# Layer B's values by way of DRAM: one write per block, then one read per quarter of the features and group of partitions, with a new written order

## The chip, the cores and the metric

The kernel runs on one core of one Trainium2 chip. The metric is the device time of one launch in microseconds (us). A core has five instruction queues that run side by side and wait for each other by semaphores: TensorE (PE, with its weight loads PEld), VectorE (DVE), ScalarE (ACT), GpSimd (POOL) and SyncE (SP), which here issues nearly all transfers. Matrix products land in PSUM, of which there are eight banks; everything else works in SBUF, a memory of 128 partitions. DRAM is reached only by transfers.

## The reference

Four layers run in turn, A, B, A, B, each as `x = x + layer(layernorm(x))`, on 2048 positions of width 512 (32 heads of 16 features), all in bf16. Layer A is a linear attention with a softmax feature map. Layer B is a dilated local attention, and the change touches only it:

```python
W, dil = 8, 2
idx = pos[:, None] - (jnp.arange(W) * dil)[None, :]      # positions s, s-2, ..., s-14
logits = jnp.einsum("bhsd,bhswd->bhsw", q, kg) * scale   # kg, vg: k and v gathered at idx
attn = _softmax(jnp.where(mask, logits, -1e9), axis=-1)
o = jnp.einsum("bhsw,bhswd->bhsd", attn, vg)
return o.reshape(B, S, D) @ wo
```

So each position looks at eight positions, two apart, of its own past, in each head.

## The kernel before

The 2048 positions are cut into four blocks of 512. A stage is named by layer pair and block: `b1_01` is the projection of layer B, first pair, block 1. Every stage adds steps to short queues, one for each stage and engine, and a long string `_ORDER` names, in base 36, which queue gives its next step. It was found by a search outside the kernel and fixes the order of every instruction on every engine. `_CHOICE` holds one digit for each step that may run on either of two engines (for most, evictions from PSUM above all, 1 is VectorE and 0 is ScalarE), and `_SLOTS` names the buffer that each tile takes. Nothing is decided when the kernel runs: each engine works through its own list and waits where an operand or a buffer is not there yet.

Seven of the eight blocks of layer B are worked out elementwise (the eighth, block 3 of the second pair, uses TensorE in another way, by `s_e1` to `s_e4`). For one of the seven:

- `s_b1` projects: `mm` (L951) makes Q, K and V in PSUM with its 16 features cut into four quarters of four (partition = 4 times the head + the quarter, and the four features of a quarter side by side in it), and `ev` (L203 on VectorE, L205 on ScalarE) copies them to SBUF. V and K carry 16 columns of the block ahead of it (the halo; POOL copies it, L977 to L993).
- `s_b2` makes the weights: `prod` (L1043) multiplies Q by eight shifted windows of K on VectorE, `lgt` (L1050) sums over features on TensorE, `ex`, `den`, `rd` and `pt` (L1057 to L1078) make the softmax, giving PT, whose partitions are four groups of 32 heads; group g stands for the window offsets g and g + 4.
- `s_b3` applies them: `pav` (L1105) multiplies PT by Vg on VectorE, one instruction for each quarter q of the features, `mo` (L1114) sums over window offsets on TensorE, `ev` copies the sum to oT. `s_out` (L543 to L567) multiplies by the output weights, adds x, and stores or normalizes for the next layer.

Vg is V laid out anew: for quarter q and group g, the 32 partitions 32g to 32g + 31 hold that quarter of the 32 heads, shifted by 2g columns. The step `vrep(q)` (L1012) of the SP queue makes it by four transfers for the four groups, in the order 0, 2, 1, 3, each of 32 rows of 2104 elements, out of every fourth partition of V in SBUF into 32 adjoining partitions of Vg in SBUF. That is 16 transfers to a block and 112 in all. Two quarters share one of the eight large buffers ("big"), which `prod`, `pav` and layer A's tiles use as well. A step `vwr` that writes V to DRAM and a branch of `vrep` that reads it from there in one transfer for all four groups are in the code, but its option, `v_dram`, is empty, so neither runs.

The same SP queue issues, in the written order, the loads, the transposes of the normalized x (`tr`, L473, tile xnT), the round trip of layer A's scales through DRAM (L848 and L855, tile Prho), the block diagonal and DRAM traffic of the eighth block (L1226, L1232 to L1243), and the stores of the output (L567).

Of the kernel before, what the change touches and what calls it, by code (L numbers as in the profile page):

```python
# [19 lines left out]
H = 32  # L20
# [3 lines left out]
NB = 4  # L24
# [5 lines left out]
KVW = 16 + TB  # L30
VGW = 3 * KVW + TB + 8
# [31 lines left out]
4 z 1s s z i 3 1t 1u 21 z z 10 3 1t i7 1v 22 22 21 1 24 24 2p z 0 t u 13 11 15 1t 1t t 16 1w 1t 1y 12 12 12 12  # L63
1x x 1t 5 v w w 25 y 14 2f 2f 18 18 18 18 1z 2g 2c 17 6 19 18 1c 1d 39 2d 1b 1a 2d 22 22 1f 1f g 21 22 22 3a 3a
2c 2c 1f 2d 20 21 1f 22 2c 7 7 20 20 22 26 29 1g 1f 1k 39 3a 2d 2d 2d 2d 1i h 3b 2f 24 2i 1h 1e 29 1j 1l 2q 2h
27 2d 2n 3c 2o 2o 29 29 2a 39 2k 2k 3a 2k 2k 2n 2n 2n 2q 2o 2o 2r 3a 3a 2q 2q 2o 2o 2o 29 2y 2y 2l 2s 2k 2o 2z
2z 2z 2z 31 31 36 3c 33 24 36 36 28 36 2y 2y 2v 2v 2z 2v 37 36 2z 2z 2z 2f 2j 2u 2v 2b 2w 2b 2b 2b 2m 36 2m 36
2m 36 36 2m 39 3a 3b 3b 31 2v 2t 3a 31 32 4e 37 3c 34 35 39 3a 2x 2x 3c 2x 30 2x 38 38 36 38 38 3i 3c 3b 3c 3c
3c 7 3d 3e 3e 3j 3k 3k 3b 3k 3c 3l 5h 3m 3n 3m 3d 3e 3d 3l 5i 3o 3m 3e 3e 3l 3p 3m 3q 3r 3m 3m 5j 3d 3v 5i 3e 3e
3s 3e 20 20 20 20 3t 3m 5h 3u 5n 3m 3m 5m 3d 3e 7c 5h 5q 5o 5p 5r 5k 5i 3f 3g 3g 7 3f 3g 3g 5l 3m 5i 5i 7d 3w 3x  # L70
5i 5i 3z 5i 5i 3f 3f 7e 5i 5s 3g 3y 3g 40 41 7d 5w 42 7f 41 41 7f 41 5t 7f 3g 5v 3g 5u 5x 44 43 45 bd 43 43 46
43 47 5y 3f 43 47 48 90 5x 5x 4b e 49 4c 60 61 41 41 4a 41 41 3g 5x 5z 5z 4d 4g 4g 4h 5z 62 5z 4l 4l 4l 91 92 7d
7d 7g 63 4i 5z 91 4f 4n 4q 4q 4m 4q 63 66 67 64 65 7j 7i 7h 4l 7k 4r 93 4g 4g 4j 4w 4w 7l 7l 4o 4w 7o 68 4k 4q
4u 93 93 4t 4s 4f 7l 7p 7m 7n 4p 4v 7n 7l 7q 6p 6k 6k 4v 6k 7n 7n 91 91 6f 6g 7r 6n 6m 6k 6a 6a 4w 94 6l 7n 69
7r 7u 6o 7v 96 7t 97 4x 95 7s 7w 98 4x 4x 4x 6f 6c 6h 4y 4y 6a 6d 6b 6r 6r 99 6f 6i 6r 99 3h 99 99 9d 9e 3h 6f
6j 6a 6e 9a 9b 9c 9b 6r 9b 9b 83 7y 7y 84 9f 9b 8d 7z 6s 6s 6s 9f 9h 6s 6t 6t 88 89 9i 7y 6s 6t 4w 4x 83 83 6q
6q 7y 6q 85 88 4y 88 8b 83 9g 87 86 81 b2 9j 9k 88 8c 9m 9n 8f 9w 9x 82 9w 9w a1 6r 9z 69 6u 9w 80 6u 6v 8a 6u
6v 6x 6v 4w 6w 6q 6u 6v 6y 9m 4v 4z 4z 6z 4v 70 71 4z 4z 70 70 9y 72 7x 73 72 74 70 75 72 72 76 9o 9r 9r 50 51
8f 50 50 72 52 76 78 8e 8e 50 53 77 54 9r 9u 79 7a 9m 9p 7b 8f 9s 9t 55 8e 56 57 8f 55 58 55 55 59 8g 8g 8g 8e
a0 8g 57 57 a3 9r 5a 57 9v 9m 9q 5b a3 57 5b 8h 8h 5c b3 5e 5d 5f 5g 7x 9l a2 b0 b0 a3 b1 b1 b1 8g 8h b1 b3 b3  # L80
b6 b3 b7 bz c0 c0 a4 a4 a4 a3 a4 a5 a5 bz c0 c0 bz d3 b4 bz c0 c0 c0 c0 8f 8i b0 b1 a4 8i 8i 8i a5 as at b0 b1
b1 bx ap a2 b5 b1 ap 8j 8k 8j 8j 8l 8m 8j bx 8n 8o a3 a6 a2 a6 8p 8o 8o 8o bx aq aq aq aq by by by 8q 8t 8r 8s
as 8q a2 as as bx a6 a7 8q 8q a7 by 8u bz 8q a6 8u 8w 8y by by aw av 8v a7 8x a8 a7 aa ap ap a9 ab ac b8 b8 au
ac i7 ac ac by by bx b8 b8 ad aq aq af aq aq ag b9 bo c0 8z ah b8 bb bb ae ae ae ae ai be ax ae ai aj an c1 be
bc bb bc bc ak ax bc bb bc bc bc bc ac ac am ax ac ax ay al ac bg be bm bm ao bm bm bj bn bn bn bn bn bn ar ax
az az az bu bu bu bu az bn bn c2 bv bj bj by bu bj bu ba ba ba ba bp bh bp bp c1 bq bk bs br be c1 c1 bu bu bu
# [12 lines left out]
ih ic dz ic dw ii ii fi ij gr gr gt ij ik ij ij fj fj ik il ga gu il in gs fl ii ij ij gv ii fj fj im ij ij ik
il ik fn fo gr gr il gw gx iq io iq iq gv gw gv gw gv gv ip iq iv dx dx fk fm fm gy gz h2 is gw gw ir it h2 iw  # L100
iu h0 it ix iw h3 h3 h4 h5 h6 h2 h1 h3 h7 h2 h5 h3 h8 h5 h5
"""


_CHOICE = (
    "0010110111100111111111000000100000100110011100000111011110010100000101010000100000000000111101011100"
    "1010010100001100100000000000000011111110000100001010100000000000000000010111001000001101000000000000"
    "1010000011111100000000000100010110011011010100101111000000001001000000010110010001000100011100100000"
    "00000000011111010000011100000000000000000000000001000011001000000000000000001100"
)  # L110


_SLOTS = {
    "med": (
        "0123456789abcdef346aff72ffc3105f92b4de6a7fd92b317ef99962c0517dbf2e3abf6925cd13e273a31dad901d74235cdb"
        "f72a94d35c017b9264acf31d08"
    ),
    "ps": (
        "0123124350123021456715604156734153267234701623047237452365001230210345672135304675261473045672350146"
        "1401230453013042567103651251741023452036714302310345031240230435406703203501467012012457245201240310"  # L120
        "3245602750235102563740130473024567142362047540123640760437034563745101021345067241301456701236204531"
        "7024560124567326452016435735601247351204561203460750264012312301203405367136731421432102324567467556"
        "47554701213740542010"
    ),
    "big": (
        "012345670123456012345617234561720351724361720436170425361725362503421034210354276"
    ),
    "t2": (
        "0123455500111123334555555555555555000002123402222222221314504555545555444455223000000145523333333333"
        "333333301045234102"  # L130
    ),
    "pp": (
        "640620202020"
    ),
}

# [1 line left out]
class _Fast:  # L138
# [804 lines left out]
    def s_b1(self, L, b):  # L943
        nc, add = self.nc, self.step
        st = "b1_%d%d" % (L, b)
        T = {}
# [52 lines left out]
        def vrep(dl):  # L999
            if dl == 0:  # L1000
                self.Vg[L, b] = {}
            if dl % 2 == 0:
                self.Vg[L, b][dl // 2] = self.big([2, NB * KVW], "Vg")
            if (L, b) in _OPT["v_dram"]:
                a = self.VD[L, b][dl:dl + 1, 2:3]
                src = bass.AP(a.tensor, a.offset, [[2, 4], [4 * NB * KVW, H], [1, VGW]])
                nc.sync.dma_start(out=self.Vg[L, b][dl // 2][:, dl % 2, 0:VGW], in_=src)
                return
            for g in (0, 2, 1, 3):
                a = T["V"][dl:dl + 1, 0:1, 2 + 2 * g:3 + 2 * g]  # L1010
                src = bass.AP(a.tensor, a.offset, [[4 * a.ap[0][0], H], [1, VGW]])
                nc.sync.dma_start(out=self.Vg[L, b][dl // 2][32 * g:32 * g + 32, dl % 2, 0:VGW], in_=src)  # L1012

        if b:
# [507 lines left out]
class _Layout:  # L1522
# [578 lines left out]
```

## Time and profile before

| | |
|---|---|
| median of 3 runs | 328.9 us (328.38 to 330.63) |
| profiled execution | 329.39 us, of which the span of the profile is 327.7 us |
| mean granted TensorE clock | 0.994 |
| transfers of V to Vg | 112 of 131.5 KB, median 4.8 us from issue to landing |

The page of the profile covers one execution. Its first part gives the busy time of each engine, its second the span in 40 equal slices (8.2 us each): one digit for each engine and slice, the busy share in tenths; below them the clock that TensorE was granted, the busy share of the 16 transfer engines, and what they moved. A view by windows gives the same for any stretch. A busy TensorE is not TensorE at its peak, since its products are pipelined.

### The profile page before, as it was taken

Reading aid. Unit: us, or ns where it says so; the run is one execution under the profiler, and the core shown is the slowest. Engines: PE = TensorE matmul, PEld = TensorE weight load, DVE = VectorE, ACT = ScalarE, POOL = GpSimd, SP = SyncE. Lnnn points to the kernel's source line nnn. Section 1 sums busy time; section 2 is a strip of 40 time slices with the busy share of each in tenths; the row PEclk is TensorE's granted clock in tenths of the full one; section 3 lists DMA queues with packets and bytes.
Section 4 is the critical chain, followed back from the end, with each engine's and each line's share of the span. In section 5 each row is a group of like instructions: output and inputs, shape, how many; then the busy total and the mean of one; then the engine's idle time right before and its main releaser. Section 6 shows DMA issues by size and latency. Waiting matters only on the chain.

```text
span 327.7 us, 8877 instructions
## 1 busy us (share of the span) xinstructions
PE 308.8 (94%) x3542; PEld 153.5 (47%) x3574; DVE 296.3 (90%) x456; ACT 278.1 (85%) x640; POOL 39.1 (12%) x64
## 2 busy tenths in 40 slices
PE   7999999899999999999999999789999999986993
PEld 3644456444444454444444455543545444443441
DVE  6899995989999999999999999599898999999493
ACT  4999989999789977999999999799898866987360
POOL 6000000000020006000000000000040395210000
PEclk9999999999999999999999999999999999999799
DMA  7964300023677979679991200050588997549814
GB/s 203 341 162 90 108 2 4 2 68 81 144 172 140 132 149 158 108 131 131 145 121 28 40 0 4 4 141 9 145 147 121 192 136 131 135 83 176 158 67 137
DMA packets 45793, 36.41 MB, mean 111 GB/s; under 512 B 30832, under 2 KB 41136, under 8 KB 45744
## 3 DMA queue, kind: packets, MB, share of 16 engines
q1 hardware_dynamic: 45216, 35.75, 56.2%
q8 instruction: 30, 0.49, 0.7%
q14 instruction: 19, 0.16, 0.2%
q10 hardware_dynamic: 528, 0.02, 0.1%
HBM read 11.13 MB, written 3.25 MB: 44 GB/s over the span
## 4 chain that ended last, share of the span: by engine, by line
DVE 31%; ACT 31%; PE 18%; issue 12%; DMA 3%; SPq 2%; DVEq 0%; ACTq 0%
DVE prod L1043 6%; ACT Eq L729 5%; DVE pav L1105 5%; PE PS L543 5%; ACT sqd L563 5%; ACT Ek L622 4%; DVE x L556 4%; DVE Ek L674 3%; PE PS L951 3%; DVE xn L466 3%; ACT oT L205 2%; PE PS L1050 2%; DVE s L649 2%; ACT xn L468 2%; DMA wraw<-in_A_wqkv_dram 1%
## 5 line engine op out<-in xcount | busy, mean ns | idle before, releaser
L951 PE MATMUL PS<-xnT,WB 128*128 128x512 bf16 x336 | 76.7, 380 | 0.3 <-ACT K L205 0.2
L1105 DVE TENSOR_TENSOR pav<-PT,Vg 128x4096 bf16<-128x4096 bf16 (+1 forms) x29 | 63.3, 2219 | 0.6
L1043 DVE TENSOR_TENSOR prod<-QT,K 128x4096 bf16<-128x4096 bf16 x28 | 62.9, 2285 | 0.4 <-ACT QT L205 0.3
L951 PEld LDWEIGHTS <-WB 128*128 128x128 bf16 x336 | 37.3, 114 | 37.1 <-issue 4.2
L543 PEld LDWEIGHTS <-oT 128*128 128x128 bf16 x240 | 22.5, 98 | 31.3 <-issue 5.6
L729 ACT ACTIVATE Eq<-PS 128x512 bf16<-128x512 f32 x64 | 34.7, 624 | 0.0
L622 ACT ACTIVATE Ek<-PS 128x512 bf16<-128x512 f32 x64 | 33.9, 627 | 0.0
L563 ACT ACTIVATE sqd<-x 128x512 bf16<-128x512 bf16 x48 | 30.4, 633 | 2.1 <-DVE x L556 1.2
L721 PE MATMUL PS<-xnT,WA 128*128 128x512 bf16 x128 | 31.1, 380 | 0.2 <-ACT bs L870 0.2
L543 PE MATMUL PS<-WoB,oT 128*128 128x512 bf16 x105 | 27.7, 393 | 3.1 <-issue 2.9
L616 PE MATMUL PS<-WA,xnT 128*128 128x512 bf16 x124 | 29.9, 379 | 0.5 <-DVE x L556 0.2
L628 PE MATMUL PS<-WA,xnT 128*128 128x512 bf16 x122 | 29.9, 379 | 0.3
L543 PE MATMUL PS<-WoA,oT 128*128 128x512 bf16 x119 | 29.3, 380 | 0.8 <-DVE x L556 0.2
L556 DVE SCALAR_TENSOR_TENSOR x<-PS,x 128x512 bf16<-128x512 f32 x45 | 28.9, 684 | 0.3 <-PE PS L543 0.2
L205 ACT CAST oT<-PS 128x512 bf16<-128x512 f32 (+1 forms) x47 | 24.8, 595 | 3.8 <-PE PS L1114 3.5
L616 PEld LDWEIGHTS <-xnT 128*128 128x128 bf16 x128 | 12.3, 98 | 15.0 <-issue 0.6
L628 PEld LDWEIGHTS <-xnT 128*128 128x128 bf16 x128 | 12.3, 98 | 14.4
L205 ACT CAST V<-PS 128x512 bf16<-128x512 f32 x27 | 15.4, 591 | 4.1 <-PE PS L951 4.1
L674 DVE TENSOR_TENSOR Ek<-Ek,rk 128x4096 bf16<-128x4096 bf16 (+1 forms) x10 | 18.6, 1860 | 0.3 <-ACT rk L669 0.3
L721 PEld LDWEIGHTS <-WA 128*128 128x128 bf16 x128 | 11.7, 97 | 15.2 <-issue 2.0
L205 ACT CAST K<-PS 128x512 bf16<-128x512 f32 x30 | 17.4, 591 | 0.3 <-PE PS L951 0.3
L466 DVE TENSOR_SCALAR xn<-x,rstd,nmr 128x512 bf16<-128x512 bf16 x46 | 16.8, 408 | 0.6
(164 smaller groups left out, 496.9 us busy)
## 6 DMA issues: line engine op xcount, KB each, us to landing
Vg<-V SPq DMA_DIRECT2D x112, 131.5 KB, 4.8
Prho<-rd SPq DMA_DIRECT2D x8, 512.0 KB, 5.4
x<-in_A_x_dram SPq DMA_DIRECT2D x3, 512.0 KB, 5.8
WB<-in_B_wqkv_dram SPq DMA_DIRECT2D x3, 512.0 KB, 8.6
out_dram<-x SPq DMA_DIRECT2D x6, 256.0 KB, 2.3
wraw<-in_A_wqkv_dram SPq DMA_DIRECT2D x4, 256.0 KB, 5.4
vd<-Vs SPq DMA_DIRECT2D x2, 272.0 KB, 3.3
x<-in_A_x_dram SPq DMA_DIRECT2D x4, 128.0 KB, 3.9
```

What stands on the lines that cost most here:

```text
L205: self.nc.scalar.copy(out=out, in_=in_)
L543: nc.tensor.matmul(y[:], lhsT=lh(t, c), rhs=Wo()[:, c, :], start=(c == 0), stop=(c == NB - 1 and not onpe))
L556: nc.vector.scalar_tensor_tensor(out=xb[:, t, :], in0=T[t][:], scalar=1.0, in1=xb[:, t, :], op0=ALU.mult, op1=ALU.add, **kw)
L563: nc.scalar.activation(out=sqd[:], in_=xb[:, t, :], func=ACT.Square, accum_out=T["ss"][:, t:t + 1])
L616: nc.tensor.matmul(pk[:], lhsT=xnT[:, t, k, :], rhs=self.WA[:, k, D:2 * D], start=(k == 0), stop=(k == NB - 1))
L622: nc.scalar.activation(out=T["E"][:, t, s, :], in_=T["k", t][:], func=ACT.Exp, scale=1.0 - 2.0 * s)
L628: nc.tensor.matmul(pv[:], lhsT=xnT[:, t, k, :], rhs=self.WA[:, k, 2 * D:3 * D], start=(k == 0), stop=(k == NB - 1))
L721: nc.tensor.matmul(pq[:], lhsT=self.WA[:, k, hb * P:(hb + 1) * P], rhs=xnT[:, :, k, :], start=(k == 0), stop=(k == NB - 1))
L729: nc.scalar.activation(out=self.Eq[L, b][s][:, :, hb, :], in_=T[hb][:].rearrange("p (t i) -> p t i", t=4), func=ACT.Exp, scale=1.0 - 2.0 * s)
L951: nc.tensor.matmul(pp[:], lhsT=self.WB[:, k, i * D + c:(i + 1) * D:NB], rhs=xnT[:, :, k, :], start=(k == 0), stop=(k == NB - 1))
L1043: nc.vector.tensor_tensor(out=pr[:], in0=QT[:, c:c + 1, :].to_broadcast([P, NW, TB]), in1=win, op=ALU.mult)
L1105: nc.vector.tensor_tensor(out=pv, in0=PT[:, :, lo:lo + n].unsqueeze(1).to_broadcast([P, NB, 2, n]), in1=vw, op=ALU.mult)
```

## The change

The option and the branch go. For all seven blocks `vwr` now writes V with its halo to DRAM in one transfer (128 partitions of 2112 elements, 540 KB), and `vrep(q)` makes the same four transfers of 32 rows for groups 0, 2, 1, 3, with the DRAM copy as their source. A read has to wait until the write has landed. Tile and instruction shapes on the computing engines stay as they are. `_ORDER`, `_CHOICE` and `_SLOTS` are replaced by ones searched for this form, so that nearly every instruction stands at another place of its queue, and some evictions, normalizations and residuals change their engine.

```diff
     "split": ((1, 2), (1, 3)),
-    "v_dram": (),
     "half_mo": (),
...
 _ORDER = """
-8 2e a d c 23 i i i 0 j 9 k j l i 2 i i i i 0 b o p i f 2 0 1m 1m 1o m n i i i i 1n 1m 1m 1p 1q 1m 1r o q r 1m t
...
+8 i i i i i i i i i i i 0 a e 9 j 2 0 b k j o p 23 0 t i i l 1m 2 1m o q i r m 0 t 1n u 1o 3 1t s 1u t 1m x 1m
...
@@ -1001,14 +1000,9 @@
                 self.Vg[L, b] = {}
             if dl % 2 == 0:
                 self.Vg[L, b][dl // 2] = self.big([2, NB * KVW], "Vg")
-            if (L, b) in _OPT["v_dram"]:
-                a = self.VD[L, b][dl:dl + 1, 2:3]
-                src = bass.AP(a.tensor, a.offset, [[2, 4], [4 * NB * KVW, H], [1, VGW]])
-                nc.sync.dma_start(out=self.Vg[L, b][dl // 2][:, dl % 2, 0:VGW], in_=src)
-                return
             for g in (0, 2, 1, 3):
-                a = T["V"][dl:dl + 1, 0:1, 2 + 2 * g:3 + 2 * g]
-                src = bass.AP(a.tensor, a.offset, [[4 * a.ap[0][0], H], [1, VGW]])
+                a = self.VD[L, b][dl:dl + 1, 2 + 2 * g:3 + 2 * g]
+                src = bass.AP(a.tensor, a.offset, [[4 * NB * KVW, H], [1, VGW]])
                 nc.sync.dma_start(out=self.Vg[L, b][dl // 2][32 * g:32 * g + 32, dl % 2, 0:VGW], in_=src)
 
         if b:
@@ -1024,8 +1018,7 @@
             add(st + "kh", "POOL", halo)
         if b < 3:
             add(st + "v", "POOL", vhalo_out)
-        if (L, b) in _OPT["v_dram"]:
-            add(st + "v", "SP", vwr)
+        add(st + "v", "SP", vwr)
         for dl in range(4):
             add(st + "v", "SP", vrep, dl)
```

More of the change, by code (lines that the diff above doesn't have):

```diff
@@ new lines @@
+7d 4g 4g 63 5z 4i 4l 4n 63 67 65 66 64 93 4q 4q 93 93 4j 4w 4w 4t 7g 4g 68 7i 4l 4q 4f 4s 4l 7h 91 91 4k 7k 7j
+4p 4u 7l 7l 7o 7m 4o 6p 7l 7p 7l 7q 3h 94 98 96 97 6a 95 6a 6a 6b 99 99 4w 7n 7n 7n 7n 6c 6f 6f 4w 6g 7r 7n 7r
+7t 7v 7s 9c 6a 7u 9a 9b 9b 99 bo 9d 4v 4v 4v 4v 4v 7w 6h 99 9e 6r 9b 9b 9f 9b 6f 6i 6f 4x 4x 6d 6j 8d 4f 4x 4x
+6k 6l 6e 6k 6m 4y 6r 4y 6k 6k 6o 6n 69 6q 69 9f 9h 9j 9g 6r 4w 9i 9k i7 83 7y 7y 80 4x 6r 6s 6s 6s 7z 4y 6s 6t
+6t 7y 81 7y 6s 6t 3h 88 89 88 83 8a 7x 9w 9x 82 9m 9m 9o 4w 9m 9n 84 8f 83 86 85 88 88 8c 83 87 9p 6q 6q 8b 6r
@@ L110 @@
+    "0001000011111100000000000010010110110011010101010011100000010000000000000110010001000000010101000100"
+    "00000000011111001000011111000000000000000000000000000011000000000000000000000100"
 )
 _SLOTS = {
-    "med": (
[L115 to L123, printed above, removed]
+    "ps": (
+        "0120341250674523106435123467304716230176423072140127143517201341230456724013567142034562317056472310"
+        "2314052316370132012456734025013467501234504623465712032145123143567102403450210210210452102415213421"
+        "0231405605231026542165215236213567156042071402607160170170261206415012012345647012350467151623017245"
+        "3401260123456074367012306273451207345234514230231231230201204250143153605612701405467137245401501454"
+        "23670163701241542301"
+    ),
@@ L124 @@
+    "med": (
+        "0123456789abcdef0043332369a01b3578cdef4293c5deaa0f3c9d214b66af50ed2c659beda10ff2fcbbbed5f78b023ca1b6"
+        "970ed3ca675fbe129ad3c06754"
     ),
     "big": (
[L126 removed]
+        "012345670123456723457230451723046172041573214573214506321406325061325631205310574"
     ),
     "t2": (
[L129 removed]
@@ L130 @@
-        "333333301045234102"
+        "0123455550000011113244444444444444444450513241111111110304521555545551541455533300221145530000000000"
+        "000000021425345014"
     ),
     "pp": (
-        "640620202020"
+        "062626262604"
     ),
```

79 lines of the change are left out of this document (36 added, 43 removed).

## The prediction

> **What bounds the kernel now.** I read the page first: its busy times and its slices.
>
> ```profile
> span 327.7 us, 8877 instructions
> ...
> PE 308.8 (94%) x3542; PEld 153.5 (47%) x3574; DVE 296.3 (90%) x456; ACT 278.1 (85%) x640; POOL 39.1 (12%) x64
> ...
> DVE  6899995989999999999999999599898999999493
> ...
> PEclk9999999999999999999999999999999999999799
> DMA  7964300023677979679991200050588997549814
> ```
>
> Three engines are nearly full, and no transfer queue can be the bound alone, with DMA at 0 in seven slices. DVE's digits are 9 from slice 7 on with few breaks: 5 at slices 6 and 25 (layer A's exponentials, ACT's work), 4 at slice 37, the tail. The view by windows says how full the elementwise part of the first layer B is:
>
> ```profile
> 100.00:120.00 20.00, 19.71 (x122) 9.55 (x113) 18.98 (x24) 18.62 (x41) 0.55 (x2) 1.00 0.90 137
> 120.00:140.00 20.00, 19.86 (x136) 9.15 (x137) 19.79 (x16) 17.36 (x41) 5.88 (x5) 1.00 0.75 133
> 140.00:160.00 20.00, 19.81 (x136) 8.86 (x137) 19.47 (x15) 19.84 (x52) 0.15 (x1) 1.00 0.95 141
> 160.00:180.00 20.00, 19.77 (x165) 8.69 (x166) 19.64 (x23) 19.87 (x47) 1.19 (x3) 1.00 0.64 84
> 200.00:210.00 10.00, 9.17 (x252) 5.72 (x251) 7.16 (x13) 7.61 (x18) 0.00 (x0) 1.00 0.01 3
> 300.00:310.00 10.00, 7.33 (x175) 3.90 (x176) 5.21 (x6) 4.07 (x13) 0.00 (x0) 0.83 0.97 180
> ```
>
> The columns after the length are PE, PEld, DVE, ACT and POOL busy, the granted clock, the DMA share and GB/s. From 100 to 180 us DVE idles 2.1 of 80 us: here time is DVE's work plus what DVE waits. From 300 to 310 us nothing is full but DMA. So the change can act in three ways: less or more work in DVE's queue, a DVE wait for Vg, and the tail.
>
> **The work that moves between engines.** Counting both written orders, instruction by instruction, DVE loses four copies of oT, two of vaug and half a one of kvT, and gains one each of K and xnT, two normalizations xn, one residual x, and one product Eq from PSUM in place of one from SBUF. ACT takes the mirror image.
>
> ```profile
> L203 DVE CAST oT<-PS 128x512 bf16<-128x512 f32 x14 | 9.4, 682 | 0.0
> L466 DVE TENSOR_SCALAR xn<-x,rstd,nmr 128x512 bf16<-128x512 bf16 x46 | 16.8, 408 | 0.6
> L556 DVE SCALAR_TENSOR_TENSOR x<-PS,x 128x512 bf16<-128x512 f32 x45 | 28.9, 684 | 0.3 <-PE PS L543 0.2
> L839 DVE TENSOR_TENSOR Eq<-PS,Eq 128x512 bf16<-128x512 f32 x18 | 11.7, 681 | 0.0
> L839 DVE TENSOR_TENSOR Eq<-bs,Eq 128x512 bf16<-128x512 bf16 x14 | 5.7, 416 | 0.1
> L205 ACT CAST oT<-PS 128x512 bf16<-128x512 f32 (+1 forms) x47 | 24.8, 595 | 3.8 <-PE PS L1114 3.5
> L468 ACT ACTIVATE xn<-x,nmr,rstd 128x512 bf16<-128x512 bf16 x18 | 14.3, 814 | 1.7 <-DVE nmr L457 1.7
> ```
>
> DVE: 4.5 copies fewer, net of the two gained and taking all at oT's 0.682, is -3.1; xn +0.8; x +0.7; Eq +0.3. Sum **-1.3 us**. ACT: four copies more by 0.595, +2.4; two xn fewer, -1.6; a net residual fewer at about a copy's 0.6; sum +0.2, nothing. PE loses one product. So the new order's gain in work is small, and only in DVE's queue.
>
> **The transfers.** The old ones and their nearest relatives, in the page's part on DMA issues and the view of the tile Vg:
>
> ```profile
> Vg<-V SPq DMA_DIRECT2D x112, 131.5 KB, 4.8
> Prho<-rd SPq DMA_DIRECT2D x8, 512.0 KB, 5.4
> out_dram<-x SPq DMA_DIRECT2D x6, 256.0 KB, 2.3
> vd<-Vs SPq DMA_DIRECT2D x2, 272.0 KB, 3.3
> xnT<-xn SPq DMA_TRANSPOSE x11, 4.6
> ```
> ```profile
> L1012 SPq DMA_DIRECT2D Vg<-V x112: 467/592/1782, 91.9 to 304.1; - x112
> ...
> DMA to landing us min/median/max: 2.8/4.8/8.2
> ```
>
> The last number of an issue row is the median from issue to landing; the tile view gives ns that SP takes to issue one (least, median, most). The number of these transfers stays 112; what is added is seven writes of 540 KB, and in front of each block's 16 reads a wait for the write. No row shows such a write. Below stands out_dram's 2.3 us; above, Vs's 3.3 us plus the other 268 KB at the slow rate of the next fence, 135 GB/s, 2.0 us: 5.3. I take 4.4, Vs's 3.3 plus 268 KB at the 247 GB/s at which Prho's rows, as long as these, move there. The rate of the copies themselves:
>
> ```profile
> 106.00:108.00 2.00, 2.00 (x11) 1.03 (x10) 2.00 (x4) 1.97 (x3) 0.00 (x0) 1.00 1.11 135
> 88.00:90.00 2.00, 2.00 (x11) 1.00 (x10) 2.00 (x2) 0.42 (x1) 0.00 (x0) 1.00 0.91 247
> ```
> ```profile
> 118.59 15.74 SPq L1012 DMA_DIRECT2D Vg<-V  x20
> 142.48 5.31 SPq L1012 DMA_DIRECT2D Vg<-V  x8
> ```
>
> SBUF to SBUF, with the engines' share at 1, they move 135 GB/s, while Prho out of DRAM moves 247 (into 128 partitions, not 32). SP's own rows give one copy in 0.66 us (5.31 / 8) to 0.79 us (15.74 / 20), against 0.59 to issue one. A read from DRAM is thus between 0.59 and 0.97 us apart (131.5 KB / 135 GB/s); I take 0.59, because its source is Prho's. [...]
>
> So from V's last eviction to a landed Vg: write 4.4; the first quarter's four reads, last issued 3 x 0.59 later and landed after 2.8 to 4.8: **9.0 to 11.0 us**. The sixteenth: 4.4 + 15 x 0.59 + 2.8 to 4.8 = **16.1 to 18.1**. [...]
>
> **Where that is late.** What covers it is the work standing in DVE's queue between V's eviction and `pav`. For blocks 01 and 11 the new order leaves 5 to 8 us less of it than the old one, two or three large products, although there is now a write to wait for.
>
> ```profile
> L1105 DVE TENSOR_TENSOR pav<-PT,Vg 128x4096 bf16<-128x4096 bf16 (+1 forms) x29 | 63.3, 2219 | 0.6
> L1043 DVE TENSOR_TENSOR prod<-QT,K 128x4096 bf16<-128x4096 bf16 x28 | 62.9, 2285 | 0.4 <-ACT QT L205 0.3
> L1078 DVE TENSOR_TENSOR PT<-E,rden 128x1024 bf16<-128x1024 bf16 x7 | 4.8, 691 | 0.6 <-ACT rden L1073 0.4
> ```
>
> The new order: block 01 has three `prod`, two `pt`, a copy of K and three xn: 3 x 2.29 + 2 x 0.69 + 0.68 + 3 x 0.41 = 10.1 us. First quarter needed at 10.1 (landed at 9.0 to 11.0), the fourth three `pav` later, at 16.8 (16.1 to 18.1): a wait of 0 to 1.3, take **0.6**. Block 11 has block 10's four `pav` and one `pt`, 4 x 2.22 + 0.69 = 9.6; fourth at 16.2: 0 to 1.9, take **0.9**. Blocks 00, 02, 03 and 10 have from 15 to 36 us of such work ahead of the first quarter, and 22 or more ahead of the fourth: hidden under `prod` and other blocks' `pav`, until that cover shrinks by some 4 us. What is behind the wait: SP holds the transpose of block 02's xn behind block 00's sixteen reads, where the old order let it in after eight copies. 4.4 + 16 x 0.59 + 4.6 (xnT's landing) = 18.4 us after V, while the first K product of block 02 stands 18 us of DVE work later: 0 to 1, take **0.3**, since PE has block 01's V there. Behind block 11's reads stand nine of the 16 Qbd transfers for the eighth block; its products come after block 11's `pav` begins, with block 12's projections ahead of them, so nothing, at most the 4.4 us of the write where PE has no other work left.
>
> **The tail.** Rows of the timeline of ACT, PEld and DVE, of the chain of waits, two windows of 1 us, and the transfers from 299.5 to 303 us:
>
> ```profile
> 292.86 0.59 ACT L205 CAST V<-PS 128x512 bf16<-128x512 f32 x1
> 302.62 0.53 PEld L543 LDWEIGHTS <-oT 128*128 128x128 bf16 x3 [2.61 <-issue]
> 302.75 2.29 DVE L1105 TENSOR_TENSOR pav<-PT,Vg 128x4096 bf16<-128x4096 bf16 x1
> ```
> ```profile
> 298.51 1.24 PE PS L1322 x126
> ```
> ```profile
> 303.00:304.00 1.00, 1.00 (x4) 0.39 (x3) 1.00 (x1) 0.00 (x0) 0.00 (x0) 0.55 1.06 160
> 305.00:306.00 1.00, 1.00 (x4) 0.29 (x2) 0.04 (x1) 0.00 (x0) 0.00 (x0) 0.50 1.05 168
> ```
> ```profile
> q8 instruction: 1, 0.02, 2.6%
> ```
>
> Block 12's V is out at 293.45 and its first `pav` starts at 302.75, 9.3 us later, on PT, not Vg. The new order has about the same work of PE there; against 9.0 to 11.0 the wait is 0 to 1.7, take **0.9**. In those 9 us lies a gap of 2.61 us of PE with no releaser, behind 126 short products in 1.24 us, while a 0.02 MB piece of instructions is under way with DMA at a share of 1; then the clock is near 0.50 for 3 us, another 1.5 lost. I read it as PE out of instructions. The new order has three groups of 64 such products in a row where the old had two, with Vg in flight too, so I keep the gap: no term.
>
> **Sum.** -1.3 (DVE) + 0.6 + 0.9 + 0.3 + 0.9 = +1.4 on the profiled execution's 329.39 us: 330.8. That execution lies 0.5 above the median of its runs (328.9), so **330.3 us**, in practice no change. With every read at its lower and upper landing the waits are 0 to 5.9, hence 327.6 to 333.5.
>
> **Rivals**, each counted from 328.9.
> 1. *Slow reads, slower than before.* If 32 partitions of a destination, and not an SBUF source, set the 135 GB/s, the reads stay 0.79 apart as in the 20 of the timeline. Fourth quarter: 4.4 + 15 x 0.79 + 4.8 = 21.1 us; late by 4.3 at block 01 and 4.9 at 11, and the first quarter by 2.3 at the tail: 11.5 - 1.3, about **339**. It decides from a pitch of about 0.67 (with a landing of 3.8, the waits then come to 4.6 us, one per cent above the work saved). For it: the 20 copies ran slower than that. Against: Prho's 247.
> 2. *Reads that free the queue.* At 247 GB/s the 16 reads are done in 8.5 us, the DMA share at the dense products falls, and the gap of 2.6 and the slow clock's 1.5 go with it: -1.3 - 4.1, **323.5**. For it: the gap stands only where DMA is full; against: the new order puts more short products in a row.
> 3. *All hidden* (the change does not reach what ends last). DVE had 0.6 us of idle before all `pav`; if ACT delivers V earlier than its place suggests, only -1.3 is left: **327.6**.
> 4. *The new order loses elsewhere.* Every buffer and nearly every place changed; one more gap as at 200 to 210 us, where DVE idles 2.8 of 10, on top of my +1.4 gives 333; two give 336. I take **334**.
>
> **How the numbers follow.** Forecast 0.38, slow reads 0.21, free queue 0.17, hidden 0.13, lost elsewhere 0.11. The range has to take in most of the free queue and of the slow reads, so 323.5 to 338.0. One per cent is 3.3 us, about what a measurement can tell from no change. Faster by more (under 325.6): nearly all of rival 2, a part of 3, 0.22. Slower by more (over 332.2): rivals 1 and 4, and some of the forecast, 0.35. Between: 0.43.
>
> **What would show it.** Vg<-vd's landing and SP's pitch over 16 reads: 0.59 to 0.66 for me, 0.79 for rival 1. DVE's wait for Vg before L1105 (new line 1098): 2 to 3 us in all, at blocks 01, 11 and 12. vd<-V: 4.4 us. PE's gap without releaser past 290 us: kept, or gone with a clock of 1.00 (rival 2). DVE's busy time: 295.0. I am wrong in kind if DVE waits elsewhere, or if a transpose of xn ends a wait of PE by more than 1 us.

## The result and the profile after

The changed kernel takes 332.2 us in the median of 19 executions, the kernel before 328.6 in the same series. Two of the 19 were disturbed (335.3 and 337.3 us); without them the median is 331.9 us (329.7 to 334.2), and all that follows is compared in this way. The ratio is **1.0098, 95% interval 1.0073 to 1.0123**. The forecast was 330.3, no change; the result is slower by one per cent, at the edge of that. The profiled execution took 333.58 us. Its page, the parts that answer those shown of before:

```profile
span 331.8 us, 8908 instructions
...
PE 313.1 (94%) x3573; PEld 152.9 (46%) x3573; DVE 295.2 (89%) x453; ACT 278.7 (84%) x642; POOL 42.3 (13%) x64
...
PEclk9999999999999999999999999999999999979799
...
q1 hardware_dynamic: 46224, 39.53, 45.1%
...
L1098 DVE TENSOR_TENSOR pav<-PT,Vg 128x4096 bf16<-128x4096 bf16 (+1 forms) x29 | 63.3, 2217 | 3.9 <-DMA Vg<-vd 3.6
...
Vg<-vd SPq DMA_DIRECT2D x112, 131.5 KB, 3.2
...
vd<-V SPq DMA_DIRECT2D x7, 528.0 KB, 3.0
```

DVE's work fell by 1.1 us, the span grew by 4.1. DVE now waits for Vg, 3.6 us in three places. But each transfer became faster: a copy lands in 3.2 us where it took 4.8. The row q1 gives packets, MB and share of the 16 engines' time; the kernel before has

```profile
q1 hardware_dynamic: 45216, 35.75, 56.2%
```

so 3.8 MB more were moved in 11 points less of the engines' time. The clock has two dips to 7 in the last eight slices, where it had one. Where they are, in windows of 2 us (PE, PEld, DVE, ACT, POOL, clock, DMA share, GB/s), with TensorE's two longest waits ahead of them:

```profile
PE PS L1315 <- issue: 2.2, 1, 2.2
PE PS L1271 <- DMA Qbd<-Qs: 2.1, 1, 2.1
```
```profile
294.00:296.00 2.00, 2.00 (x50) 0.91 (x31) 2.00 (x2) 1.86 (x5) 0.00 (x0) 0.62 0.68 110
296.00:298.00 2.00, 2.00 (x6) 0.76 (x5) 2.00 (x2) 0.89 (x3) 1.05 (x1) 0.53 0.21 61
...
308.00:310.00 2.00, 2.00 (x67) 1.20 (x68) 1.81 (x3) 0.61 (x3) 0.00 (x0) 0.53 0.87 283
310.00:312.00 2.00, 2.00 (x7) 0.78 (x6) 2.00 (x2) 0.60 (x1) 0.00 (x0) 0.61 0.51 176
```

Each wait is followed by about 4 us in which TensorE has some 0.57 of its clock: 1.7 us lost each time, beside the wait itself. This execution has both, and its mean clock is 0.990; the mean clocks say that others have less of it. Of after's executions, those with a mean clock of 0.996 or more took 329.7 to 331.1 us, those from 0.992 to 0.995 took 330.7 to 332.6, those with 0.991 or less 332.3 to 334.2.

### The profile page after: what moved, and what is told of

Its sections match the earlier page's. It is cut to its first block, busy times and chain, and to the rows that moved or that the text cites. A ratio compares the mean times of both kernels' runs of the same rounds, so it can differ in the third digit from the quotient of the medians.

```text
span 331.8 us, 8908 instructions
## 1 busy us (share of the span) xinstructions
PE 313.1 (94%) x3573; PEld 152.9 (46%) x3573; DVE 295.2 (89%) x453; ACT 278.7 (84%) x642; POOL 42.3 (13%) x64
## 3 DMA queue, kind: packets, MB, share of 16 engines
q1 hardware_dynamic: 46224, 39.53, 45.1%
## 4 chain that ended last, share of the span: by engine, by line
PE 54%; ACT 16%; DVE 14%; DMA 6%; SPq 4%; issue 4%; DVEq 0%; ACTq 0%
PE PS L950 13%; PE PS L542 9%; PE PS L627 6%; PE PS L720 6%; DVE pav L1098 5%; PE PS L615 5%; DMA Vg<-vd 4%; ACT Eq L728 3%; PE PS L1043 3%; ACT sqd L562 3%; SPq L1006 2%; DVE x L555 2%; ACT Ek L621 2%; ACT oT L204 2%; DMA wraw<-in_A_wqkv_dram 2%
## 5 line engine op out<-in xcount | busy, mean ns | idle before, releaser
L950 PE MATMUL PS<-xnT,WB 128*128 128x512 bf16 x336 | 78.1, 383 | 0.3
L542 PEld LDWEIGHTS <-oT 128*128 128x128 bf16 x240 | 23.2, 100 | 31.5 <-issue 4.7
L728 ACT ACTIVATE Eq<-PS 128x512 bf16<-128x512 f32 x64 | 33.9, 615 | 0.0
L542 PE MATMUL PS<-WoA,oT 128*128 128x512 bf16 x128 | 30.0, 379 | 1.6 <-DVE oT L202 1.5
L204 ACT CAST oT<-PS 128x512 bf16<-128x512 f32 (+1 forms) x51 | 27.5, 596 | 4.6 <-PE PS L1107 3.9
L555 DVE SCALAR_TENSOR_TENSOR x<-PS,x 128x512 bf16<-128x512 f32 x46 | 29.7, 683 | 1.5 <-PE PS L542 1.4
L615 PE MATMUL PS<-WA,xnT 128*128 128x512 bf16 x128 | 30.4, 379 | 0.0
L627 PE MATMUL PS<-WA,xnT 128*128 128x512 bf16 x128 | 30.4, 379 | 0.0
L542 PE MATMUL PS<-WoB,oT 128*128 128x512 bf16 x112 | 29.6, 401 | 0.1
L465 DVE TENSOR_SCALAR xn<-x,rstd,nmr 128x512 bf16<-128x512 bf16 x48 | 17.6, 415 | 0.6
L1107 PE MATMUL PS<-pav,indAV 128*32 128x512 bf16 (+1 forms) x232 | 15.1, 374 | 2.2 <-DVE pav L1098 2.1
```

What stands on the lines that cost most here:

```text
L204: self.nc.scalar.copy(out=out, in_=in_)
L542: nc.tensor.matmul(y[:], lhsT=lh(t, c), rhs=Wo()[:, c, :], start=(c == 0), stop=(c == NB - 1 and not onpe))
L555: nc.vector.scalar_tensor_tensor(out=xb[:, t, :], in0=T[t][:], scalar=1.0, in1=xb[:, t, :], op0=ALU.mult, op1=ALU.add, **kw)
L615: nc.tensor.matmul(pk[:], lhsT=xnT[:, t, k, :], rhs=self.WA[:, k, D:2 * D], start=(k == 0), stop=(k == NB - 1))
L627: nc.tensor.matmul(pv[:], lhsT=xnT[:, t, k, :], rhs=self.WA[:, k, 2 * D:3 * D], start=(k == 0), stop=(k == NB - 1))
L728: nc.scalar.activation(out=self.Eq[L, b][s][:, :, hb, :], in_=T[hb][:].rearrange("p (t i) -> p t i", t=4), func=ACT.Exp, scale=1.0 - 2.0 * s)
```

## The experiments

Line numbers shift a little between the kernels, since lines are added or left out. Times are medians beside the kernel before on the same chip, which stood at 328.6 to 328.7 in the first three sets and at 329.2 in the last run.

**Path and order, crossed.** The change has two halves, and each can be had alone.

```diff
 # new_order_sbuf: the new order, the old path
-        add(st + "v", "SP", vwr)
-                a = self.VD[L, b][dl:dl + 1, 2 + 2 * g:3 + 2 * g]
+                a = T["V"][dl:dl + 1, 0:1, 2 + 2 * g:3 + 2 * g]
 # old_order_dram: the old order; vwr's step stands directly ahead of each block's vrep(0)
+        add(st + "v", "SP", vwr)
+                a = self.VD[L, b][dl:dl + 1, 2 + 2 * g:3 + 2 * g]
```

> The changed kernel's order, engines and buffers, with the old path: no write, the 16 copies of a block out of V in SBUF. It tells the order from the path. The changed kernel stands at 332.2 us in the median, the kernel before at 328.6. Theory O (the new order is the loss, the path is about free): 331 to 333, DVE's idle before pav changed by less than 1 us from 3.6. Theory H (the hop through DRAM is the loss): the wait for Vg goes to below 1 us and the time to 328 to 330. Theory P (the path is a gain, since a read takes SP 0.42 us against 0.59 for an old copy, and the order needs it): slower than the changed kernel, 334 to 338, DVE's wait for Vg 5 us or more.

> The order, engines and buffers of the kernel before, with the new path: one write per block put directly ahead of its first read in SP's queue, all 112 reads from DRAM. Theory O and theory P (the path is free or a gain): 326 to 329, with DVE's wait for Vg below 1 us and SP's reads 0.42 to 0.55 apart. Theory H (the hop costs where it is put): 331 to 334, with 2 us or more of DVE waiting for Vg. If the gap of 2.6 us in PE past 299 us comes from full transfer engines, it is shorter than 1 us here, and the time falls to 325.

| | copies out of SBUF | through DRAM |
|---|---|---|
| old order | 328.7 (before) | 325.9, ratio 0.9908 [0.9887, 0.9929] |
| new order | 347.1, ratio 1.0533 [1.0494, 1.0572] | 331.9 (after) |

The path is a gain in both rows, 2.8 and 15.2 us. The order is the loss in both columns, 18.4 and 6.0 us. In the new order the old copies are far too late for DVE, and cost much more than Theory P's 334 to 338; in the old order the new reads are never late (its list of DVE's waits has no row for `pav`):

```profile
DVE pav L1081 <- DMA Vg<-V: 16.9, 11, 2.7
```

The new order needs the faster copies, and does less well with them than the old one. Where its 6.0 us lie is seen by setting the profiles of the two kernels with the new path side by side, in the timeline of DVE (start, length, instruction, count), after first, then old_order_dram:

```profile
83.48 4.49 DVE L1036 TENSOR_TENSOR prod<-QT,K 128x4096 bf16<-128x4096 bf16 x2
...
120.25 18.03 DVE L1098 TENSOR_TENSOR pav<-PT,Vg 128x4096 bf16<-128x4096 bf16 x8 [2.44 <-DMA Vg<-vd]
...
241.85 4.49 DVE L1036 TENSOR_TENSOR prod<-QT,K 128x4096 bf16<-128x4096 bf16 x2
...
289.30 8.94 DVE L1036 TENSOR_TENSOR prod<-QT,K 128x4096 bf16<-128x4096 bf16 x4
```
```profile
84.01 6.69 DVE L1021 TENSOR_TENSOR prod<-QT,K 128x4096 bf16<-128x4096 bf16 x3
...
125.22 11.41 DVE L1083 TENSOR_TENSOR pav<-PT,Vg 128x4096 bf16<-128x4096 bf16 x5
...
241.12 2.32 DVE L1021 TENSOR_TENSOR prod<-QT,K 128x4096 bf16<-128x4096 bf16 x1
...
293.60 2.29 DVE L1083 TENSOR_TENSOR pav<-PT,Vg 128x4096 bf16<-128x4096 bf16 x1
```

| after each had done | after | old_order_dram | difference |
|---|---|---|---|
| nothing yet of layer B | 83.5 | 84.0 | -0.5 |
| nine `prod`, eight `pav` | 138.3 | 136.6 | +1.7 |
| all of the first layer B, layer A again | 241.9 | 241.1 | +0.7 |
| twelve `prod` and eight `pav` of the second | 298.2 | 295.9 | +2.3 |
| everything (span) | 331.8 | 325.3 | +6.5 |

The wait of 2.4 us at block 01 is there, but of the 1.7 lost by then 1.0 is won back by 241 us. About two thirds of the loss, 4.2 us, comes in the last 34 us. The stretches of slow clock, 1.7 us each in this profile of after, weigh in that: the executions with a mean clock of 0.997 or more stand at 330.9 us (five of after) and 325.5 (three of old_order_dram), 5.4 apart. So the order's loss is more than the clock.

**The tail of the new order.** Qbd is the block diagonal that the short products of the eighth block read; Vs, WA and Vx are that block's values on their way to DRAM and back, and oB is its output, made by DVE. Nine of the 16 Qbd transfers stand behind block 11's reads, the last seven of them mixed with three writes of Vs and a load of WA. From SP's timeline of after:

```profile
275.21 7.64 SPq L1006 DMA_DIRECT2D Vg<-vd  x16
...
284.86 1.61 SPq L1228 DMA_DIRECT2D vd<-Vs  x1
...
290.96 1.22 SPq L1219 DMA_DIRECT2D Qbd<-Qs  x2
```

From 275.2 us SP issues almost without a pause, and the last Qbd goes out at 291.6. The wait is not new in kind; the kernel before has one of half the length:

```profile
PE PS L1278 <- DMA Qbd<-Qs: 1.0, 1, 1.0
```

The next kernel moves the seven ahead of the writes. In the lines of the orders, `qsc` is a Qbd transfer, `vwr` and `vwh` write Vs, `vrd` loads WA, `mo` is a group of 64 short products.

```diff
 # new_qbd_first, in SP's order near 284 us
- vwr(0) vwh qsc(1) vwr(1) qsc(2..5) vrd(0,0) qsc(6) qsc(7)
+ qsc(1..7) vwr(0) vwh vwr(1) vrd(0,0)
 # new_qbd_split, on top of it: PE's third group of 64 short products
- mo mo mo  out(block 11, 0)  out(1)
+ mo mo  out(block 11, 0) mo  out(1)
```

> The changed kernel with one thing moved in SP's queue: the last seven of the sixteen Qbd transfers of the eighth block go ahead of its three writes of Vs, one of which waits for ACT. Theory T (the tail is the loss: PE waits 2.1 us for Qbd near 291 us and then runs at half clock for 4 us): PE's wait for Qbd falls below 0.5 us, the clock from 294 to 298 us is 1.0, and the time falls by 2.5 to 4, to 328 to 330. If the tail waits next for what stands behind it (the loads of WA and Vx, the gap of 2.2 us near 306): 331 to 332.

> The changed kernel with Qbd moved ahead (329.9 us alone, its runs from 328.2 to 334.1) and the third of the three groups of 64 short products that stand in a row moved behind one output product of block 11. Theory C (the rest of the new order's loss is PE's second gap with the half clock that some executions have behind it): 327.5 to 328.8, all runs within 1.5 us of each other. Rival W (the rest is what DVE waits before 298 us, and PE for Vx): 329.5 to 330.5, no change from 329.9.

new_qbd_first: 329.8 us (ratio 1.0057 [1.0027, 1.0086]). In its profile the wait for Qbd and the first half clock are gone. Against after that is 2.0 us by the medians, and 1.4 by the ratios to the kernel before and also among the executions of both with a mean clock of 0.997 or more (330.9 and 329.5): the only edit of the new order that won anything. TensorE then waits for the next thing that SP had put last, in the view of its weight loads:

```profile
304.04 1.67 PEld L1299 LDWEIGHTS <-et 128*32 128x32 bf16 x189 [2.25 <-DMA Vx<-vd]
```

new_qbd_split: 332.3 us (1.0118 [1.0083, 1.0152]); the gain is given back, although its profiled execution, at a clock of 0.999, took 330.1. The forecast of 327.5 to 328.8 missed. One group moved does not free TensorE: a gap as long stands in front of the output products, and the profile gives DVE's `oB` as its end.

```profile
305.52 0.55 PEld L526 LDWEIGHTS <-oT 128*128 128x128 bf16 x4 [2.36 <-issue]
```
```profile
PE PS L526 <- DVE oB L1326: 2.3, 1, 2.3
```

So of the order's 6.0 us the place of the Qbd transfers explains 1.4 to 2.0. What makes up the rest was not taken apart by any run.

**Block 01's wait.** Is it the hop through DRAM? One kernel lets the reads take rows of the input x, so that none waits for the write; another puts the first eight reads ahead of a transpose that stands between write and reads; a third adds the Qbd edit to that.

```diff
 # new_no_hop
-                a = self.VD[L, b][dl:dl + 1, 2 + 2 * g:3 + 2 * g]
-                src = bass.AP(a.tensor, a.offset, [[4 * NB * KVW, H], [1, VGW]])
+                a = self.A_x
+                src = bass.AP(a.tensor, dl * NB * KVW + 2 + 2 * g, [[4 * NB * KVW, H], [1, VGW]])
 # new_early_reads, in SP's order
- vwr(01)  tr(block 03)  vrep(01, 0) vrep(01, 1)  vrep(01, 2) vrep(01, 3)
+ vwr(01)  vrep(01, 0) vrep(01, 1)  tr(block 03)  vrep(01, 2) vrep(01, 3)
```

> The changed kernel, but the 112 reads take their rows from the input x in DRAM, at the same strides and sizes, so that none waits for the write of V (the write stays, and layer B's values are not V: this leaves out the dependence). It measures the hop alone. Theory H: DVE's wait for Vg falls from 3.6 us to below 0.5 and the time by 2.5 to 4, to 328 to 330. Theory O or a loss in the tail (PE's wait of 2.1 us for Qbd, the gap of 2.2 us and the half clock behind each): DVE's wait falls too, but the time by at most 1.5, to 331 to 332.

> The changed kernel with the first eight reads of block 01 (quarters 0 and 1) moved ahead of the transpose of block 03's xn in SP's queue. The changed kernel stands at 332.2 us. Theory S (SP is held by that transpose, whose issue takes 4.04 us when it stands directly behind a write, so the reads start at 115.3 and not when the write has landed, near 113.5): the reads start before 114.5, the transpose takes about 2 us to issue, DVE's wait before block 01's first pav falls from 2.44 us to 0.4 to 1.2, and the time by 1.2 to 2, to 330.2 to 331. Rival: the wait is only moved, because the transpose now comes late for block 03's projections: PE waits 1 us or more for xnT near 120 us and the time stays at 332.

> Both edits on the changed kernel: block 01's first eight reads ahead of the transpose, and the last seven Qbd transfers ahead of the writes of Vs, which alone gave 329.9 us. If the two losses add (they stand 170 us apart, and DVE has work all the way between them): 328 to 329. If DVE's gain at block 01 is used up before the tail, since an engine other than DVE ends layer A's second half: 329.9, as with Qbd alone. In both cases above the 325.9 of the old order with the new path, because the second half's other waits stay.

SP's timeline around 111 us (write, transpose, reads) in after, in new_no_hop and in new_early_reads:

```profile
110.41 0.35 SPq L996 DMA_DIRECT2D vd<-V  x1
111.08 4.04 SPq L472 DMA_TRANSPOSE xnT<-xn  x1
115.30 7.85 SPq L1006 DMA_DIRECT2D Vg<-vd  x16
```
```profile
110.56 0.35 SPq L980 DMA_DIRECT2D vd<-V  x1
111.23 4.38 SPq L456 DMA_TRANSPOSE xnT<-xn  x1
115.74 7.96 SPq L990 DMA_DIRECT2D Vg<-in_A_x_dram  x16
```
```profile
111.38 0.35 SPq L980 DMA_DIRECT2D vd<-V  x1
116.45 3.85 SPq L990 DMA_DIRECT2D Vg<-vd  x8
120.42 2.95 SPq L456 DMA_TRANSPOSE xnT<-xn  x1
```

The write's own row in the view of transfers, for after and new_early_reads (the last number is us to landing):

```profile
vd<-V SPq DMA_DIRECT2D x1, 528.0 KB, 4.8
```
```profile
vd<-V SPq DMA_DIRECT2D x1, 528.0 KB, 5.0
```

Two things end together in after: the write, landed 4.8 us after its issue (the others in 2.6 to 3.7), and the transpose, which holds SP for 4.04 us (another, at 101 us, for 1.8). Without the first (new_no_hop) the second still holds the reads to 115.7; without the second the write alone holds them to 116.45, 5.1 us after its issue. DVE's wait stays in both, 2.4 us and, in two parts, 2.0 and 3.1:

```profile
DVE pav L1082 <- DMA Vg<-in_A_x_dram: 2.8, 2, 2.4
```
```profile
120.76 4.54 DVE L1082 TENSOR_TENSOR pav<-PT,Vg 128x4096 bf16<-128x4096 bf16 x2 [1.98 <-DMA Vg<-vd]
128.44 6.82 DVE L1082 TENSOR_TENSOR pav<-PT,Vg 128x4096 bf16<-128x4096 bf16 x3 [3.14 <-DMA Vg<-vd]
```

new_no_hop takes 330.8 us (1.0081 [1.0047, 1.0115]), not told apart from after: the wait for the write is not what the new order's time hangs on. new_early_reads takes 335.4 (1.0197 [1.0177, 1.0218]) and with the Qbd edit 337.2 (1.0215 [1.0171, 1.0260]): here the rival was right that the wait is only moved, to TensorE, in a size that I had not expected.

```profile
PE PS L934 <- DMA xnT<-xn: 6.0, 1, 6.0
```

The transpose now comes some 8 us later, TensorE has nothing else in its order, and everything behind it shifts. With the two ratios' intervals overlapping, the Qbd edit has no effect here that can be told. In new_early_reads one more transfer was under way with the slow write, a piece of instructions:

```profile
q8 instruction: 1, 0.02, 2.2%
```

In after (there of 0.01 MB) and new_no_hop such a piece went beside the same write too, and beside none of their other six. But in old_order_dram a write beside such a piece, at 92.0 us, landed in 2.9 us, and in new_early_reads another, at 136 us, in 3.6, so why that one write is slow stays open. A kernel that takes both causes away was not tried, so what block 01's wait is worth stays open.

**Where the path's gain is.** Two rows of DVE's timeline in the kernel before stand beside those of old_order_dram above:

```profile
240.87 2.33 DVE L1043 TENSOR_TENSOR prod<-QT,K 128x4096 bf16<-128x4096 bf16 x1
...
293.75 2.28 DVE L1105 TENSOR_TENSOR pav<-PT,Vg 128x4096 bf16<-128x4096 bf16 x1
```

Each pair is at most 0.25 us apart; the gain comes after 294 us. So block 12 alone was sent through DRAM, and in another kernel its copies were left out altogether (GpSimd writes zeros into its Vg, so V is missing from that block's output).

```diff
 # old_dram_last
+                if (L, b) == (1, 2):   # read from VD, written by vwr for this block only
 # before_no_copy_12
+            if (L, b) == (1, 2):
+                if dl % 2 == 0:
+                    nc.gpsimd.memset(self.Vg[L, b][dl // 2][:], 0.0)
+                return
```

> The kernel before, with the new path for the last elementwise block (12) alone; the other six blocks copy out of SBUF as before. The new path in all seven blocks gave 325.9 against 328.7. Theory L (the path's gain lies in the tail: up to the prod at 284 us both profiles stand within 0.3 us of each other, and the half clock behind PE's gap is gone): 326 to 327, clock 1.0 from 303 to 306 us. Rival E (every block gives its part, or the earlier ones prepare the tail by SP being free for Qbd): 328 to 328.5, and PE's wait of 1.0 us for Qbd near 287 us stays.

> The kernel before, whose last elementwise block (12) has no copies of V at all: GpSimd writes zeros into its Vg instead (two writes of 2 x 2112 elements per partition), so that block's output leaves out V. It takes the transfers under PE's gap away and leaves the products as they are; the new path for block 12 alone gave 326.3 us, the old one 328.7. Theory D (the SBUF copies under way lengthen the refill of PE's instructions, and the longer gap is what brings the half clock): the gap is at most 2.1 us, as with the new path, clock 1.0, 325.5 to 326.5. Theory R (a refill takes its 2 to 2.6 us whatever else is under way, and the new path's gain came from another place): a gap of 2.3 us or more and 327.5 to 329. If the gap goes below 1 us: a refill without load is hidden, 324 to 325.5.

| block 12's Vg | gap of PE behind the short products | DMA share, 300 to 302 us | clock behind it | time |
|---|---|---|---|---|
| out of SBUF (before) | 2.61 | 1.04 | 0.50 | 328.7 |
| DRAM, all blocks (old_order_dram) | 2.37 | 0.54 | 1.00 | 325.9 |
| DRAM, block 12 alone | 2.04 | 0.59 | 1.00 | 326.3, 0.9924 [0.9906, 0.9942] |
| no copies | 1.39 | 0.00 | 1.00 | 326.4, 0.9926 [0.9896, 0.9955] |

The rows behind the table, from the view of weight loads and from windows of 2 us, for before (whose gap the prediction shows), old_order_dram, old_dram_last and before_no_copy_12:

```profile
300.00:302.00 2.00, 0.07 (x1) 0.01 (x1) 1.67 (x3) 1.91 (x6) 0.00 (x0) 1.00 1.04 175
```

```profile
301.70 0.53 PEld L527 LDWEIGHTS <-oT 128*128 128x128 bf16 x3 [2.37 <-issue]
...
300.00:302.00 2.00, 0.30 (x2) 0.18 (x2) 1.97 (x5) 1.09 (x3) 0.00 (x0) 1.00 0.54 160
302.00:304.00 2.00, 2.00 (x14) 0.74 (x16) 2.00 (x1) 0.00 (x0) 0.00 (x0) 1.00 0.88 267
```
```profile
301.90 0.53 PEld L527 LDWEIGHTS <-oT 128*128 128x128 bf16 x3 [2.04 <-issue]
...
300.00:302.00 2.00, 0.11 (x1) 0.10 (x1) 1.99 (x4) 1.62 (x5) 0.00 (x0) 1.00 0.59 164
```
```profile
302.11 0.53 PEld L527 LDWEIGHTS <-oT 128*128 128x128 bf16 x3 [1.39 <-issue]
...
300.00:302.00 2.00, 1.00 (x56) 0.56 (x43) 2.00 (x5) 1.91 (x9) 2.00 (x1) 1.00 0.00 0
```

Nearly the whole gain, 2.4 of 2.8 us, comes from one block of seven. Leaving its copies out gives no more, but that profile begins the gap 0.7 us later than the kernel before does (300.7 against 300.0), and waits before it, 0.7 us of DVE for QT near 291 among them, use up a part of what the gap wins. In these four profiles the gap is longest with SBUF copies under way, and only the longest has the half clock behind it. In all four one piece of 0.02 MB of instructions is moved within 1.2 us of the gap's start.

The half clock is not what the path wins, though. In the profile of before it costs 1.7 us (clocks of 0.78, 0.50 and 0.87 in the three windows from 302 to 308 us). But of the kernel before's 59 executions in these sets the ten with a mean clock of 0.998 or more, which cannot have lost half of that, took 328.3 us in the median (327.1 to 328.9), the other 49 took 328.7. Without the half clock the old path still stands 2.4 us above old_order_dram. What those ten wait for in its place no profile shows, so how block 12's transfers cost their 2.4 us stays open.

**Is it the gap?** If so, cutting the burst of short products should do as much as the path. The second group of 64 was moved behind two of block 11's output products, with the new path and with the old, and behind one.

```diff
 # old_dram_split, before_split; in old_dram_split_one only out(0) stands between
- mo mo den out(0) out(1) pt(0) pt(1)
+ mo den out(0) out(1) mo pt(0) pt(1)
```

> The old order with the new path (325.9 us), and the second of the eighth block's four groups of 64 short products moved behind two of the dense output products of block 11, its two ACT steps with it. Theory I (PE runs out of instructions: 128 short products with their weight loads are used up in 1.5 us, the piece of 0.02 MB that refills them is seen at the start of the gap, and the gap of 2.37 us lies in the middle of a run of output products that waits for nothing): the gap falls below 0.8 us and the time to 323.5 to 325. Rival C (the gap is a wait that the profile does not show, or comes from transfers under way): a gap of 2 us or more stays past 298 us, 325.5 to 327.

> The kernel before (old order, all seven blocks copied out of SBUF), with the eighth block's second group of 64 short products behind two output products of block 11: only PE's gap of 2.55 us past 299.9 us is taken away, not the path. It tells what the path's gain in the tail was. Theory G (the gain is the half clock behind the gap, 3 us at 0.5, and every cure of the gap gives it): 326 to 327.5, clock 1.0 from 303 to 308 us. Theory D (the gain is less load on the transfers of block 12 and what follows them): 328 to 329, as before, although the gap is gone, since block 12's Vg then lands late or oB is waited for.

> The old order with the new path (325.9 us), the second group of 64 short products moved behind one output product of block 11 instead of two (with two: 326.5, the gap of 2.37 us gone, but PE then waited 0.9 us for oB and 0.8 without a releaser). If half the shift keeps the gap away and halves the wait for oB: 324.8 to 325.7. If the refill of instructions needs more than one dense product of 0.9 us: the gap is back at 1 us or more, 325.5 to 326.5.

The gap goes where the burst is cut, and others open: in old_dram_split, then in before_split, a wait of 1.21 us for oB and this one:

```profile
305.51 0.40 PEld L1300 LDWEIGHTS <-et 128*32 128x32 bf16 x41 [0.94 <-issue]
```
```profile
307.54 0.40 PEld L1306 LDWEIGHTS <-et 128*32 128x32 bf16 x41 [1.76 <-issue]
```

With the new path that is a draw: 326.5 us (0.9924 [0.9905, 0.9943]) and, with one product, 325.8 (0.9925 [0.9899, 0.9951]). With the old path it is a loss, 330.9 us (1.0069 [1.0046, 1.0093]): the same second gap is 1.76 us instead of 0.94, and all but two of its executions ran at a mean clock of 0.994 or less; those two, at 0.998 and 1.000, took 328.8 and 328.0. So my theory that any cure of the gap gives the path's gain is wrong: these two have neither that gap nor a slow clock, and stand where the kernel before stands. With the lighter transfers the gap was shorter at both places where it was seen (2.37 us against 2.61, 0.94 against 1.76); cutting one burst only moved its gap.

**The best version** is old_order_dram, 325.9 us: the new path on the old order, 0.9% faster than the kernel before and 1.9% faster than the changed one.

## Why the prediction was right in the number and wrong in its parts

- *The work moved* was right: -1.3 us forecast for DVE, 295.2 against 296.3 measured.
- *The write* was over-sized: 4.4 us forecast, 3.0 in the median (six of 2.6 to 3.7 and the one of 4.8). That the reads wait for its landing shows at blocks 00 and 02, where SP issues nothing between them: it goes out at 89.05 and 126.76 us and lands after 2.7 and 3.7, and the first read goes out at 91.81 and 130.57.
- *The reads* were under the range that I gave them. Where they stand alone, 16 reads take SP 7.64 to 8.78 us, 0.48 to 0.55 apart (five blocks of seven), below my least 0.59; SP issues one in 0.42 us in the median, where a copy took 0.59:

```profile
L1006 SPq DMA_DIRECT2D Vg<-vd x112: 302/420/1676, 91.8 to 307.5; - x112
```

  With 3.2 to land, a sixteenth is there 3.0 + 15 x 0.49 + 3.2 = 13.6 us after V, not 16.1 to 18.1. Rival 1, the slow reads, falls with that. What it would have cost was under-sized: new_order_sbuf, with the old copies' pace and no write to wait for, took 347 us, not 339. That the reads from DRAM are the lighter transfers is shown by the shares above (45.1% of the engines' time for 39.53 MB, against 56.2% for 35.75 MB with SBUF copies); 332 against 347 us in one and the same order agrees with it.
- *DVE's waits for Vg* came to 3.6 us in all, against 2.4 forecast at three blocks, but not as forecast. Block 01 has 2.4 us (0.6 forecast); block 11 has 0.8 (0.9 forecast); the tail has none (0.9 forecast), since PT is later still; 0.3 stands in the first layer at 171.6 us. At block 01 the landing was as forecast and the cover was not. V's last eviction ended at 110.34 us:

```profile
109.21 1.13 ACT L204 CAST V<-PS 128x512 bf16<-128x512 f32 x2
```

  The first quarter was there at 120.25, 9.9 us later, inside 9.0 to 11.0, though by luck: a slow write and a transpose, which the forecast had only for block 02's xn, where it cost nothing, made up for the faster reads. But DVE was ready for `pav` at 117.81, after 7.5 us and not 10.1. By then it had only two of the three `prod` that I counted and none of the three xn, with 0.8 us of waiting for rden: the place in the written order is not the time at which ACT delivers V. That less cover stands here was read rightly off the order; how much was not.
- *"Behind block 11's reads stand nine of the 16 Qbd transfers … so nothing"* is the step that failed most clearly. TensorE waited 2.1 us for the last of them, and in the profiled execution the half clock came on top: 1.4 to 2.0 us by new_qbd_first. The products do come after block 11's `pav`, as I said, but SP, issuing without a pause, reached the last of these transfers only at 291.6 us: I had counted the nine, and not the 7.6 us of reads and 3.2 us of writes and a load ahead of them and between them (0.58 + 1.61 + 0.53 + 0.46). The kernel before's own wait of 1.0 us at this place was there to be read.
- *The tail's gap kept* was right for the new order, 2.29 against 2.61 us, but that is no constant: on the old order the profile with the new path has a shorter one, 2.37 us, and a full clock behind it. That is the direction of rival 2 (323.5; 325.9 measured without the new order), and its condition, transfer engines that are less full, goes with a shorter gap in before_no_copy_12 too. Its other half, that the whole gap would go, is wrong: 1.4 us remain in before_no_copy_12, with a DMA share of 0.00. Nor is the slow clock the 1.5 us that I and rival 2 counted: over many executions of the kernel before it makes about 0.5.
- *The sum* had the path as a cost (+2.7) and the order as a small gain (-1.3). It is the other way: path -2.8, order +6.0. Rival 4 (the new order loses elsewhere, 334) is nearest to what happened; a gain of the kind of rival 2 stood against it, on the old order at least. That 330.3 came near 331.9 is luck: +1.4 and +3.2 are both small sums of terms of opposite sign, and mine had the signs the wrong way round. I had not thought of pricing the two halves apart, each against the old other half.

## What to carry to other kernels

Where a change brings a new data path and a new schedule together, price and run the four combinations: here each half was several times the net effect, and the better kernel was one that nobody had written. Follow each transfer through its queue up to its issue, past every instruction ahead of it that holds the queue: for the last Qbd that was 16 us (from 275.2 to 291.6), against 2.0 us to land. A transfer can be worth more than its own wait: no `pav` waited for Vg in either kernel of the old order, and the lighter transfers still gave 2.8 us.

## What the runs showed of the hardware that I had not expected

- The half clock is not a matter of one length of gap. Behind PE gaps of 2.61 us (before), 2.23 and 2.29 (after) the clock fell to 0.5 to 0.6 for 3 to 4 us; behind 2.37 (old_order_dram), 2.25 (new_qbd_first, mean clock 0.997) and 2.36 (new_qbd_split) it stayed at 1.00. Executions of one kernel differ in it: new_qbd_first's took 328.2 to 329.5 us at a mean clock of 0.997 or more, and 329.8 to 332.4 below. What goes with it differs too: 2 to 3 us in the time of these, about 0.5 us in the kernel before. What decides whether the clock falls no run here shows.
- In the profiles of before, after, old_dram_last, new_qbd_split and before_no_copy_12 a PE gap of 1.39 to 2.61 us stands behind 126 to 128 short products with as many weight loads, taken in 1.2 to 1.5 us; with the burst cut, gaps of 1.08 and 1.38 us stand behind 60 and 87 of these loads (old_dram_split_one). A piece of 0.02 MB of instructions is under way between 299.5 and 300 us in before, between 305 and 306 in after and between 299.5 and 300 in before_no_copy_12; the gaps begin at 300.0, 305.7 and 300.7. If the gap is the wait for that piece, it was 1.4 us with a DMA share of 0.00 and 2.6 us with SBUF copies under way. That the piece is the cause is argued from this, not shown by a run of its own, and one thing speaks against it: another such piece, at 305 us in before and at 306.5 in old_dram_last, has no gap of more than 0.9 us near it.
- A transpose issued right behind a write of 528 KB (540 thousand bytes) held SP for 4.0 to 4.4 us at block 01 in three profiles (after, new_no_hop, new_qbd_first) and for 3.4 to 3.5 at 257 us. Of the others between 84 and 180 us in the same profiles the first, behind the loads of Prho, took 2.7 to 3.0, and the rest 1.7 to 2.0.
